# Batch 0's first attention part reordered around the transposes, q and k loaded and cast ahead of v, and feed-forward units metered by a carried credit

## The chip, the cores and the metric

The kernel runs on one core of a Trainium2 chip. The metric is the device time of one execution in microseconds; the time before is the median of three runs.

## The reference, cut to what matters

```python
def _attn_ref(q, k, v, is_retrieval, n_sink, window):      # 4 batches, 8 heads, 768 positions, depth 64
    scores = scale * np.matmul(q, k.transpose(0, 1, 3, 2))
    ...
    stream_keep = causal & (is_sink | in_win)              # 4 sinks, window 64
    mask = np.where(retr[0, :, 0, 0, None, None], full_mask, stream_mask)
    ...
    return np.matmul(a, v).astype(np.float32)              # a: softmax of the masked scores

def _moe_ref(x, w_in, w_out, alpha):                       # 3072 tokens, 512 -> 2048 -> 512
    h = x @ w_in
    g = np.maximum(h, 0.0) + alpha * np.minimum(h, 0.0)
    return (g @ w_out).astype(np.float32)
```

Heads 0, 2 and 6 are retrieval heads (causal mask), the other five are streaming heads (sinks and window). The attention output, heads side by side, is the x of the feed-forward part.

## The kernel before, in words

Every engine executes its instructions in the order in which the source emits them; the order is written by hand and nothing reorders it.

Attention is cut into segments of one batch and two heads. Batch 0 is split: segments 0 to 3 (kind "a", "part one") cover its first 512 positions, segments 4 to 7 (kind "b") the other 256. Segments 8 to 19 (kind "all") are the head pairs of batches 1 to 3. The fourth pair of each batch is two streaming heads, the other pairs one of each kind.

One segment goes like this. `load(n)` issues the DMAs of q, k and v (float32). `cast(n)` makes bf16 copies on POOL: `qb`, `kb` and, for v, `vb`, whose column of ones and empty tile `clear_v` has set. `Tq` and `Tk` transpose q and k on PE into one PSUM bank each, from which ACT (q of part one) or DVE (k, in one copy for a retrieval head, in three for a streaming head) copies them to `qT` and `kT`. The padding of `kT` is zeroed at the start by `clear_k`, each buffer on an engine of its own. `S_retr` and `S_stream` are the score pieces: matmuls into one of two score banks, then the exponential on ACT into `eR` or `eS`. In part one the mask is added on PE, by matmuls with `nmr` and `nms`; later DVE multiplies it in afterwards, with `mr`, `ms` and `ms5`. `AV(n, hh)` multiplies with `vb` and DVE divides (`rcp`, then `xn`); `X(n)` transposes the result, and DVE copies it to `xT`.

PSUM has eight banks: two for scores (`sc`), two for `AV` (`pav`), three for the feed-forward part (`mm0` to `mm2`) and a single one, `tr`, for all of `Tq`, `Tk` and `X`.

The feed-forward part is cut into units. `P1(t, f)` computes 128 of the 2048 hidden features of token tile t (512 or 256 tokens): four matmuls, a Relu on ACT (`neg`), and one DVE instruction (`g`). `P2(t, s, u)` is a quarter of the second product: four matmuls of 512 columns.

The program: loads 0 to 3; constants and clears; `cast(0)`, `Tq(0)`, `Tk(0)`; casts 1 to 3 on POOL with the issues of the weight loads `load_w_in(0..3)` and `load_w_out` between and behind them; the pieces of part one; P1 of token tile 0 (its last pair's share as soon as `X(3)` has run). Then the pieces of segments 4 to 19 follow, and after each piece as many units as a meter allows. A stage of the meter ends where a batch's last `xT` is due, and the units of the next tokens come in: tile 1 during segments 8 to 11, tiles 2 and 3 during 12 to 15, tiles 4 and 5 during 16 to 19. Tiles 6 and 7 run at the end. The meter before, with `left` the number of pieces to the end of the stage:

```python
budget = sum(c for c, _ in units) / left
while units and budget >= units[0][0] / 2:
    c, u = units.pop(0)
    budget -= c
    u()
```

Of the kernel before, what the change touches and what calls it, by code (L numbers as in the profile page):

```python
# [9 lines left out]
ALU = mybir.AluOpType  # L10
# [4 lines left out]
def kernel(  # L15
# [13 lines left out]
    nc = tc.nc  # L29
    B, H, S, D = q.shape  # L30
# [73 lines left out]

    def load(n, k_eng=None):
        sg, s = SEGS[n], n % NF
        base = (sg.b * H + sg.heads[0]) * S * D
        for src, dst, eng in ((q, qf[s], nc.sync), (k, kf[s], k_eng or nc.sync)):
            if sg.kind == "all":
                eng.dma_start(dst.rearrange("p h i d -> p (h i) d"),  # L110
                              dram(src, base, [[D, 128], [128 * D, 12], [1, D]]))
            else:

                T = (sg.q1 - sg.q0) // 128
                eng.dma_start(dst[:, :, 0:T, :].rearrange("p h i d -> p h (i d)"),
                              dram(src, base + sg.q0 * D, [[T * D, 128], [S * D, 2], [1, T * D]]))
        for hh, h in enumerate(sg.heads):
            lo, hi = sg.v_tiles(h)
            hi = min(hi, 6)
            o = (sg.b * H + h) * S * D  # L120
            step = 128 if RETR[h] else 124
            nc.sync.dma_start(vf[s][:, lo:hi, hh, :],
                              dram(v, o + lo * step * D, [[D, 128], [step * D, hi - lo], [1, D]]))
            if not RETR[h] and sg.kind != "a":
                nc.sync.dma_start(vf[s][0:24, 6, hh, :], dram(v, o + 744 * D, [[D, 24], [1, D]]))

    natq, natk = {}, {}

    def cast(n):
        sg, s = SEGS[n], n % NF  # L130
        vv = vb[sg.seq % NV]
        T = (sg.q1 - sg.q0) // 128
        if sg.kind == "b":
            natq[n], natk[n] = nat_b[0][sg.c], nat_b[1][sg.c]
        else:
            natq[n] = work.tile([128, 6, 128], bf16, tag="qb", name="qb")
            natk[n] = work.tile([128, 6, 128], bf16, tag="kb", name="kb")
        nc.gpsimd.tensor_copy(natq[n][:, 0:T, :].rearrange("p i (h d) -> p h i d", h=2), qf[s][:, :, 0:T, :])  # L138
        nc.gpsimd.tensor_copy(natk[n][:, 0:T, :].rearrange("p i (h d) -> p h i d", h=2), kf[s][:, :, 0:T, :])
        (la, ha), (lb, hb) = [sg.v_tiles(h) for h in sg.heads]  # L140
        if sg.kind == "all" or (la, ha) == (lb, hb):
            nc.gpsimd.tensor_copy(vv[:, lb:hb, :, 0:D], vf[s][:, lb:hb])
        else:
            nc.gpsimd.tensor_copy(vv[:, la:ha, 0, 0:D], vf[s][:, la:ha, 0])
            nc.gpsimd.tensor_copy(vv[:, lb:hb, 1, 0:D], vf[s][:, lb:hb, 1])
        for hh, h in enumerate(sg.heads):
            if not RETR[h]:
                lo, hi = sg.v_tiles(h)
                lo = max(lo, 1)
                vh = vv[0:NSINK, :, hh, 0:D]  # L150
                nc.gpsimd.tensor_copy(vh[:, lo:hi, :], vh[:, 0:1, :].to_broadcast([NSINK, hi - lo, D]))

    load(0, nc.scalar)
    load(1, nc.scalar)
    alpha_r = wpool.tile([16, 128], fp32, name="alpha_r")
    nc.scalar.dma_start(alpha_r, moe_alpha.rearrange("(a p) -> a p", p=128))
    load(2, nc.scalar)
    load(3)

# [11 lines left out]
    nmr = const.tile([128, 5, 144], bf16, name="nmr")  # L171
    nms = const.tile([128, 2, 192], bf16, name="nms")

# [26 lines left out]

    clear_k(nc.scalar, 1)
    clear_k(nc.vector, 0)
    nc.vector.memset(qT[0][:, SPLIT:S + 32], 0.0)
    nc.vector.tensor_copy(ms[:, 1, :], ms[:, 0, :])
    nc.vector.tensor_scalar(nms, ms, -1.0, 30000.0, op0=ALU.add, op1=ALU.mult)
    nc.vector.tensor_scalar(nmr, mr, -1.0, 30000.0, op0=ALU.add, op1=ALU.mult)
    for e in eR:
        nc.vector.memset(e[:, 1292:1612], 1.0)
        nc.vector.memset(e[:, E_R - 128:E_R], 1.0)
    clear_e(nc.vector, eS[0])  # L210
    for i in range(NV):
        clear_v(nc.vector, i)
    for i in range(1, NK):
        nc.vector.memset(qT[i][:, SPLIT:S + 32], 0.0)
    clear_k(nc.gpsimd, 2)
    clear_k(nc.scalar, 3)

# [12 lines left out]

    def T_bank(nat, n):
        tr = ps.tile([128, 1024], bf16, tag="tr", name="tr")
        for i in range(n):
            nc.tensor.transpose(tr[:, 128 * i:128 * (i + 1)], nat[:, i, :], ident)  # L234
        return tr

    def Tq(n):
        sg = SEGS[n]
        T = (sg.q1 - sg.q0) // 128
        tr = T_bank(natq.pop(n), T)  # L240
        dst = qT[sg.seq % NK][:, sg.q0:sg.q1]
# [6 lines left out]
    def Tk(n):  # L248
        sg = SEGS[n]
        T = (sg.q1 - sg.q0) // 128  # L250
        tr = T_bank(natk.pop(n), T)
        for hh, h in enumerate(sg.heads):
# [75 lines left out]
    def S_stream(n, hh, m):  # L328
# [18 lines left out]
        for j, a, z in parts + extra:  # L347
            nc.tensor.matmul(sc[:, o:o + z - a], kt[:, 128 * j:128 * (j + 1)],  # L348
                             qt[:, 124 * j + a:124 * j + z], start=True, stop=not on_pe)
            if on_pe:  # L350
                nc.tensor.matmul(sc[:, o:o + z - a], ident, nms[:, 0, a:z], start=False, stop=True)
            o += z - a
# [92 lines left out]

    def seg_pieces(n):
        sg = SEGS[n]
        parts = []
        for hh, h in enumerate(sg.heads):
            fn, m = (S_retr, sg.n_r) if RETR[h] else (S_stream, sg.n_s)  # L450
            parts.append([lambda m=m, hh=hh, fn=fn: fn(n, hh, m) for m in range(m)])
        sa, sb = parts

# [6 lines left out]

    cast(0)
    Tq(0)
    Tk(0)
    cast(1)
    load_w_in(0)
    clear_e(nc.gpsimd, eS[1])
    cast(2)
    for i in range(1, 4):
        load_w_in(i)
    cast(3)  # L470
    clear_e(nc.gpsimd, eS[2])
    clear_k(nc.gpsimd, 4)
    for i in range(NF):
# [6 lines left out]
    for n in range(8, 8 + NF):  # L480
        load(n)
    for n in range(3):
        for piece in seg_pieces(n)[0]:
            piece()
        if n == 0:

            tra = ps.tile([128, 16], fp32, tag="tr", name="tra")
            nc.tensor.transpose(tra, alpha_r, ident_f)
            nc.vector.tensor_scalar(oma, tra, -1.0, 1.0, op0=ALU.mult, op1=ALU.add)

            nc.vector.tensor_copy(ms5[:, 0, :], ms[:, 0, :])
            nc.vector.tensor_copy(ms5[:, 1, 0:148], ms[:, 0, 0:148])
            nc.vector.tensor_copy(ms5[:, 1, 148:192], ms[:, 0, 0:44])
            nc.vector.memset(ms5[0:NSINK, 1, 148:152], 0.0)
    for piece in seg_pieces(3)[0]:
        piece()
    P1(0, 0, range(3))
# [27 lines left out]
    fills = [i for i, (_, _, ready) in enumerate(pieces) if ready]  # L525
    units = p1_units(0, range(13, 16)) + p2_units(0)
    for i, (pre, piece, ready) in enumerate(pieces):
# [4 lines left out]
        if ready and i < fills[-1]:  # L532
            for _, u in units:
                u()
            units = []
            for t in ready:
                units += p1_units(t) + p2_units(t)
            continue
        if i == fills[-1]:
            break  # L540
        budget = sum(c for c, _ in units) / left
        while units and budget >= units[0][0] / 2:
# [49 lines left out]
```

## Time and profile before

| | |
|---|---|
| median of 3 runs | 276.46 us (276.16 to 276.47) |
| profiled execution | 276.85 us, its span 274.5 us |
| PE busy | 241.5 us (88% of the span) |
| DVE busy | 180.5 us (66%) |
| ACT busy | 144.8 us (53%) |
| POOL busy | 67.6 us (25%) |

The span runs from the first to the last instruction; the rest of the execution's time lies around it. Busy time is the time in which an engine had an instruction running; a releaser in square brackets is what ended the idle time before an instruction, inferred from semaphore events.

### The profile page before, as it was taken

Reading aid. Unit: us, or ns where it says so; the run is one execution under the profiler, and the core shown is the slowest. Engines: PE = TensorE matmul, PEld = TensorE weight load, DVE = VectorE, ACT = ScalarE, POOL = GpSimd, SP = SyncE. Lnnn points to the kernel's source line nnn. Section 1 sums busy time; section 2 is a strip of 40 time slices with the busy share of each in tenths; the row PEclk is TensorE's granted clock in tenths of the full one; section 3 lists DMA queues with packets and bytes.
Section 4 is the critical chain, followed back from the end, with each engine's and each line's share of the span. In section 5 each row is a group of like instructions: output and inputs, shape, how many; then the busy total and the mean of one; then the engine's idle time right before and its main releaser. Section 6 shows DMA issues by size and latency. Waiting matters only on the chain.

```text
span 274.5 us, 5621 instructions
## 1 busy us (share of the span) xinstructions
PE 241.5 (88%) x2113; PEld 150.6 (55%) x2139; DVE 180.5 (66%) x481; ACT 144.8 (53%) x307; POOL 67.6 (25%) x122
## 2 busy tenths in 40 slices
PE   0486789897998588999999899999998999999994
PEld 0365534554586465555556765555555854456551
DVE  7566578745699876699642986798436955873320
ACT  5445367553476443667534644776345744654421
POOL 7899225500451244050401312220000000000000
PEclk9999999999999989999999999999999999999998
DMA  7999999999995954961021101000111011000111
GB/s 215 275 215 213 208 224 221 221 213 250 244 251 112 175 111 101 212 146 31 0 79 39 41 0 41 38 2 1 41 76 39 4 40 39 0 2 38 76 40 76
DMA packets 75274, 29.84 MB, mean 109 GB/s; under 512 B 63968, under 2 KB 72176, under 8 KB 75248
## 3 DMA queue, kind: packets, MB, share of 16 engines
q1 hardware_dynamic: 70176, 24.51, 40.4%
q0 software_dynamic: 4224, 4.19, 9.1%
q10 hardware_dynamic: 848, 0.79, 0.9%
q8 instruction: 16, 0.26, 0.4%
q14 instruction: 10, 0.08, 0.1%
HBM read 27.39 MB, written 6.29 MB: 123 GB/s over the span
## 4 chain that ended last, share of the span: by engine, by line
PE 68%; DVE 16%; ACT 5%; DMA 3%; issue 2%; POOL 2%; SPq 1%; ACTq 0%; POOLq 0%; DVEq 0%
PE mm L414 25%; PE mm L431 20%; PE sc L431 7%; PE pav L379 5%; DVE g L421 5%; PE tr L234 3%; PE sc L316 3%; DVE xn L386 3%; PE tr L394 2%; PE sc L348 2%; ACT eR L323 2%; DMA vf<-in_v_dram 2%; ACT neg L420 2%; DVE eS L360 2%; DMA kf<-in_k_dram 2%
## 5 line engine op out<-in xcount | busy, mean ns | idle before, releaser
L414 PE MATMUL mm<-xT,w_in_b 128*128 128x256 bf16 (+1 forms) x503 | 98.2, 325 | 4.6 <-DVE g L421 3.3
L421 DVE SCALAR_TENSOR_TENSOR g<-neg,oma,mm 128x512 bf16<-128x512 f32 (+1 forms) x128 | 77.1, 611 | 23.3 <-ACT neg L420 19.9
L420 ACT ACTIVATE neg<-mm 128x512 f32<-128x512 f32 (+1 forms) x128 | 62.4, 492 | 41.8 <-PE mm L414 37.1
L431 PE MATMUL mm<-w_out_b,g 128*128 128x512 bf16 x274 | 71.5, 379 | 0.8
L414 PEld LDWEIGHTS <-w_in_b 128*128 128x128 bf16 x512 | 47.8, 98 | 34.2 <-issue 5.8
L323 ACT ACTIVATE eR<-sc 128x455 bf16<-128x455 f32 (+5 forms) x72 | 38.9, 551 | 23.2 <-PE sc L316 19.4
L431 PEld LDWEIGHTS <-g 128*128 128x128 bf16 x384 | 34.9, 98 | 26.7
L355 ACT ACTIVATE eS<-sc 128x384 bf16<-128x384 f32 x60 | 29.1, 490 | 33.4 <-PE sc L348 27.0
L138 POOL CAST qb<-qf 128x768 bf16<-128x768 f32 (+1 forms) x16 | 12.4, 777 | 84.9 <-PE tr L234 69.7
L316 PE MATMUL sc<-qT,kT 128*128 128x268 bf16 (+16 forms) x141 | 26.8, 274 | 2.1 <-DVE kT L270 1.5
L326 DVE TENSOR_TENSOR eR<-eR,mr 128x128 bf16<-128x128 bf16 (+4 forms) x60 | 14.3, 255 | 16.8 <-ACT eR L323 16.6
L360 DVE TENSOR_TENSOR eS<-eS,ms 128x384 bf16<-128x384 bf16 x50 | 18.4, 373 | 10.4 <-ACT eS L355 10.2
L431 PE MATMUL sc<-w_out_b,g 128*128 128x512 bf16 x93 | 22.9, 379 | 0.2
L386 DVE TENSOR_TENSOR xn<-pav,rcp 128x448 bf16<-128x448 f32 (+2 forms) x40 | 21.8, 544 | 1.4
L348 PE MATMUL sc<-qT,kT 128*128 128x192 bf16 (+4 forms) x150 | 21.3, 234 | 0.3 <-DVE kT L277 0.3
L316 PEld LDWEIGHTS <-kT 128*128 128x128 bf16 x141 | 12.4, 101 | 11.5 <-DVE kT L270 2.0
L435 ACT COPY ot<-mm 128x512 f32<-128x512 f32 x18 | 10.6, 586 | 14.1 <-PE mm L431 14.1
L348 PEld LDWEIGHTS <-kT 128*128 128x128 bf16 x150 | 14.0, 99 | 6.7 <-DVE kT L277 0.4
L379 PEld LDWEIGHTS <-eS 128*128 128x128 bf16 x270 | 11.8, 99 | 7.9 <-DVE eS L360 3.3
L379 PE MATMUL pav<-vb,eS 128*128 128x65 bf16 x270 | 13.5, 195 | 2.4 <-DVE eS L360 2.0
L396 DVE COPY xT<-tr 128x768 bf16<-128x768 bf16 (+2 forms) x20 | 9.5, 475 | 9.3 <-PE tr L394 9.3
L234 PE MATMUL tr<-ident,qb 128*128 128x128 bf16 x88 | 8.3, 233 | 7.9 <-POOL qb L138 5.3
(79 smaller groups left out, 207.4 us busy)
## 6 DMA issues: line engine op xcount, KB each, us to landing
out_dram<-ot SPq DMA_DIRECT2D x24, 256.0 KB
qf<-in_q_dram SPq DMA_DIRECT2D x12, 384.0 KB
kf<-in_k_dram SPq DMA_DIRECT2D x12, 384.0 KB
vf<-in_v_dram SPq DMA_DIRECT2D x24, 192.0 KB
w_in_b<-in_moe_w_in_dram POOLq DMA_DIRECT2D x4, 512.0 KB, 7.5
w_out_b<-in_moe_w_out_dram POOLq DMA_DIRECT2D x4, 512.0 KB, 12.0
qf<-in_q_dram SPq DMA_DIRECT2D x4, 256.0 KB
vf<-in_v_dram SPq DMA_DIRECT2D x5, 160.0 KB
```

What stands on the lines that cost most here:

```text
L234: nc.tensor.transpose(tr[:, 128 * i:128 * (i + 1)], nat[:, i, :], ident)
L316: nc.tensor.matmul(sc[:, a - lo:z - lo], kt[:, 128 * j:128 * (j + 1)], qt[:, c:c + z - a], start=True, stop=not masked)
L323: nc.scalar.activation(e[:, lo:hi], sc[:, 0:hi - lo], AF.Exp, scale=scale)
L348: nc.tensor.matmul(sc[:, o:o + z - a], kt[:, 128 * j:128 * (j + 1)], qt[:, 124 * j + a:124 * j + z], start=True, stop=not on_pe)
L355: nc.scalar.activation(two, sc[:, 0:384].rearrange("p (s c) -> p s c", c=192), AF.Exp, scale=scale)
L360: nc.vector.tensor_tensor(two, two, ms5 if first == 4 else ms, op=ALU.mult)
L379: nc.tensor.matmul(pav[:, i, :], e[:, o:o + 128], vv[:, j, hh, :], start=(m == 0), stop=(m == len(terms) - 1))
L386: nc.vector.tensor_tensor(xn[n][:, lo:hi, 64 * hh:64 * hh + 64], pav[:, lo:hi, 0:D], rcp[:, lo:hi].to_broadcast([128, hi - lo, D]), op=ALU ...
L414: nc.tensor.matmul(psg[:, 0:w], w_in_b[:, a, 128 * f:128 * (f + 1)], xT[:, c, o:o + w], start=(c == 0), stop=(c == 3))
L420: nc.scalar.activation(neg[:, 0:w], psg[:, 0:w], AF.Relu, scale=-1.0)
L421: nc.vector.scalar_tensor_tensor(g_buf[t % 2][:, f, 0:w], neg[:, 0:w], oma[:, f:f + 1], psg[:, 0:w], op0=ALU.mult, op1=ALU.add)
L431: nc.tensor.matmul(po[t], g_buf[t % 2][:, f, 128 * s:128 * (s + 1)], w_out_b[:, f, :], start=(f == 0), stop=(f == 15))
```

## The change

1. **Order of part one.** `Tq(n+1)` and `Tk(n+1)` come after the second score piece of segment n; `AV(n, 0)` comes last in segment n, `AV(n-1, 1)` after two score pieces of segment n, `X(n-1)` behind the first piece of the second head.
2. **Banks.** In part one `Tq` takes the bank `mm0` and `Tk` the bank `mm1`; `tr` serves `X` alone.
3. **Loads and casts.** q and k are loaded and cast apart from v: `load_qk(0)`, `(1)`, `load_v(0)`, `load_qk(2)`, and so on; k of segment 2 is issued on SP instead of ACT. The first weight load is issued after the v cast of segment 1, the last two after the v cast of segment 3.
4. **Clears and constants.** `kT` buffers 1, 2 and 3 change engines (1 from ACT to DVE, 2 from POOL to ACT, 3 from ACT to POOL); ACT's clear, and DVE's clears of `vb`, `eS[0]` and `qT[1..4]`, move behind `Tk(0)`; the second half of `ms` and with it half of `nms` leaves the start, and `ms`, `ms5` are completed after part one.
5. **Meter.** The budget is carried from piece to piece.

```diff
-    load(0, nc.scalar)
-    load(1, nc.scalar)
+    load_qk(0, nc.scalar)
+    load_qk(1, nc.scalar)
 ...
-    load(2, nc.scalar)
-    load(3)
+    load_v(0)
+    load_qk(2, nc.sync)
+    load_v(1)
+    load_qk(3, nc.sync)
+    load_v(2)
+    load_v(3)
...
-    clear_k(nc.scalar, 1)
     clear_k(nc.vector, 0)
     nc.vector.memset(qT[0][:, SPLIT:S + 32], 0.0)
-    nc.vector.tensor_copy(ms[:, 1, :], ms[:, 0, :])
-    nc.vector.tensor_scalar(nms, ms, -1.0, 30000.0, op0=ALU.add, op1=ALU.mult)
+    clear_k(nc.gpsimd, 3)
     nc.vector.tensor_scalar(nmr, mr, -1.0, 30000.0, op0=ALU.add, op1=ALU.mult)
+    nc.vector.tensor_scalar(nms, ms[:, 0, :], -1.0, 30000.0, op0=ALU.add, op1=ALU.mult)
+    clear_k(nc.vector, 1)
     for e in eR:
         nc.vector.memset(e[:, 1292:1612], 1.0)
         nc.vector.memset(e[:, E_R - 128:E_R], 1.0)
-    clear_e(nc.vector, eS[0])
-    for i in range(NV):
-        clear_v(nc.vector, i)
-    for i in range(1, NK):
-        nc.vector.memset(qT[i][:, SPLIT:S + 32], 0.0)
-    clear_k(nc.gpsimd, 2)
-    clear_k(nc.scalar, 3)
...
-        tr = T_bank(natq.pop(n), T)
+        tr = T_bank(natq.pop(n), T, "mm0" if sg.kind == "a" else "tr")
...
-        tr = T_bank(natk.pop(n), T)
+        tr = T_bank(natk.pop(n), T, "mm1" if sg.kind == "a" else "tr")
...
-    cast(0)
+    cast_qk(0)
     Tq(0)
     Tk(0)
-    cast(1)
+    clear_k(nc.scalar, 2)
+    for i in range(NV):
+        clear_v(nc.vector, i)
+    clear_e(nc.vector, eS[0])
+    cast_qk(1)
+    cast_v(0)
+    clear_e(nc.gpsimd, eS[1])
+    cast_qk(2)
+    cast_v(1)
     load_w_in(0)
-    clear_e(nc.gpsimd, eS[1])
-    cast(2)
-    for i in range(1, 4):
-        load_w_in(i)
-    cast(3)
+    cast_qk(3)
+    cast_v(2)
+    load_w_in(1)
     clear_e(nc.gpsimd, eS[2])
+    cast_v(3)
+    load_w_in(2)
+    load_w_in(3)
...
-    for n in range(3):
-        for piece in seg_pieces(n)[0]:
+    for i in range(1, NK):
+        nc.vector.memset(qT[i][:, SPLIT:S + 32], 0.0)
+    for n in range(4):
+        sa, sb = seg_scores(n)
+        first = [lambda: AV(n - 1, 1)] if n else []
+        if n < 3:
+            first += [lambda: Tq(n + 1), lambda: Tk(n + 1)]
+        seq = sa[:2] + first + sa[2:] + sb[:1]
+        seq += ([lambda: X(n - 1)] if n else []) + sb[1:] + [lambda: AV(n, 0)]
+        for piece in seq:
             piece()
...
-            nc.vector.tensor_copy(ms5[:, 0, :], ms[:, 0, :])
-            nc.vector.tensor_copy(ms5[:, 1, 0:148], ms[:, 0, 0:148])
-            nc.vector.tensor_copy(ms5[:, 1, 148:192], ms[:, 0, 0:44])
-            nc.vector.memset(ms5[0:NSINK, 1, 148:152], 0.0)
-    for piece in seg_pieces(3)[0]:
-        piece()
+    nc.vector.tensor_copy(ms[:, 1, :], ms[:, 0, :])
+    nc.vector.tensor_copy(ms5[:, 0, :], ms[:, 0, :])
+    nc.vector.tensor_copy(ms5[:, 1, 0:148], ms[:, 0, 0:148])
+    nc.vector.tensor_copy(ms5[:, 1, 148:192], ms[:, 0, 0:44])
+    nc.vector.memset(ms5[0:NSINK, 1, 148:152], 0.0)
...
-        budget = sum(c for c, _ in units) / left
+        if not ready:
+            budget += (sum(c for c, _ in units) - budget) / left
```

## Rows read from the trace of the kernel before

**Rows 1.** The page: its span, and the DMA engines' busy tenths in 40 slices.
```profile
span 274.5 us, 5621 instructions
...
DMA  7999999999995954961021101000111011000111
```

**Rows 2.** Busy time by stretch: start:end and length, engines (instructions), granted clock, DMA.
```profile
10.10:16.00 5.90, 5.08 (x43) 4.22 (x43) 2.85 (x9) 2.60 (x6) 5.77 (x13) 1.00 1.23 256
16.00:21.20 5.20, 3.90 (x56) 3.08 (x56) 2.94 (x11) 3.08 (x7) 5.14 (x12) 1.00 1.24 208
21.20:27.20 6.00, 3.87 (x60) 3.03 (x58) 3.31 (x12) 3.25 (x8) 5.53 (x14) 1.00 1.23 213
27.20:34.30 7.10, 5.20 (x66) 3.74 (x68) 4.35 (x13) 2.45 (x8) 1.89 (x7) 1.00 1.22 207
...
74.40:90.00 15.60, 14.44 (x186) 11.88 (x183) 13.90 (x40) 11.77 (x31) 5.66 (x8) 1.00 0.91 183
90.00:100.00 10.00, 6.88 (x92) 5.07 (x89) 7.70 (x25) 4.45 (x9) 2.80 (x5) 0.83 0.62 117
100.00:113.30 13.30, 11.81 (x118) 7.52 (x120) 9.78 (x28) 5.74 (x13) 4.34 (x6) 1.00 0.76 164
113.30:151.70 38.40, 38.02 (x309) 21.87 (x312) 25.42 (x62) 22.75 (x46) 7.94 (x11) 1.00 0.30 75
```

**Rows 3.** Timeline up to the first scores: start, length, engine, instruction, idle before.
```profile
2.95 1.79 DVE L204 COPY ms<-ms 128x192 bf16<-128x192 bf16 x1
3.05 1.63 POOL L189 MEMSET kT<- 128x896 bf16 x2
4.21 3.45 ACT L187 CAST kT<-zero 128x896 bf16<-128x896 f32 x4
...
5.17 0.65 POOL L139 CAST kb<-kf 128x512 bf16<-128x512 f32 x1
...
7.57 0.57 ACT L245 COPY qT<-tr 128x512 bf16<-128x512 bf16 x1
...
8.20 0.59 PE L234 MATMUL tr<-ident,kb 128*128 128x128 bf16 x4 [2.29 <-POOL vb L145]
...
9.40 0.62 DVE L270 COPY kT<-tr 64x512 bf16<-64x512 bf16 x1
...
10.08 0.54 PE L316 MATMUL sc<-qT,kT 128*128 128x430 bf16 x1 [1.30 <-DVE kT L270]
```

**Rows 4.** Timeline: weight issues, transposes around segment 1's middle, last P1 share.
```profile
14.78 2.23 POOL L223 DMA_DIRECT2D w_in_b<-in_moe_w_in_dram  x3
...
17.86 0.45 PE L394 MATMUL tr<-ident,xn 128*128 128x128 bf16 x5
...
18.83 0.38 PE L234 MATMUL tr<-ident,qb 128*128 128x128 bf16 x4 [0.52 <-POOL vb L142]
...
19.89 0.38 PE L234 MATMUL tr<-ident,kb 128*128 128x128 bf16 x4 [0.67 <-ACT qT L245]
...
34.28 0.81 PE L414 MATMUL mm<-xT,w_in_b 128*128 128x512 bf16 x3 [0.51 <-DVE xT L396]
```

**Rows 5.** Groups by line: count, busy us, mean ns of one, idle before.
```profile
L189 DVE MEMSET kT<- 128x448 uint32 x2 | 0.9, 432 | 0.1
...
L206 DVE TENSOR_SCALAR nmr<-mr 128x720 bf16<-128x720 bf16 x1 | 0.8, 751 | 0.0
...
L208 DVE MEMSET eR<- 128x320 bf16 x2 | 0.7, 325 | 0.0
...
L205 DVE TENSOR_SCALAR nms<-ms 128x384 bf16<-128x384 bf16 x1 | 0.6, 577 | 0.0
...
L492 DVE COPY ms<-ms 128x148 bf16<-128x148 bf16 x1 | 0.5, 506 | 0.0
...
L209 DVE MEMSET eR<- 128x128 bf16 x2 | 0.3, 165 | 0.0
```

**Rows 6.** The tile `w_in_b`: time from the issue of its four loads to landing.
```profile
DMA to landing us min/median/max: 6.0/7.5/10.5
```

More of the change, by code (lines that the diff above doesn't have):

```diff
@@ L103, in dram, with load, load_qk @@
         return bass.AP(t.tensor, t.offset + offset, dims)
-    def load(n, k_eng=None):
+    def load(n):
+        load_qk(n, nc.sync)
+        load_v(n)
+    def load_qk(n, k_eng):
         sg, s = SEGS[n], n % NF
         base = (sg.b * H + sg.heads[0]) * S * D
-        for src, dst, eng in ((q, qf[s], nc.sync), (k, kf[s], k_eng or nc.sync)):
+        for src, dst, eng in ((q, qf[s], nc.sync), (k, kf[s], k_eng)):
             if sg.kind == "all":
@@ L116, in load, with load_v @@
                               dram(src, base + sg.q0 * D, [[T * D, 128], [S * D, 2], [1, T * D]]))
+    def load_v(n):
+        sg, s = SEGS[n], n % NF
         for hh, h in enumerate(sg.heads):
@@ L129, in cast, with cast_qk @@
     def cast(n):
+        cast_qk(n)
+        cast_v(n)
+    def cast_qk(n):
         sg, s = SEGS[n], n % NF
-        vv = vb[sg.seq % NV]
         T = (sg.q1 - sg.q0) // 128
@@ L139, in cast, with cast_v @@
         nc.gpsimd.tensor_copy(natk[n][:, 0:T, :].rearrange("p i (h d) -> p h i d", h=2), kf[s][:, :, 0:T, :])
+    def cast_v(n):
+        sg, s = SEGS[n], n % NF
+        vv = vb[sg.seq % NV]
         (la, ha), (lb, hb) = [sg.v_tiles(h) for h in sg.heads]
@@ L171 @@
     nmr = const.tile([128, 5, 144], bf16, name="nmr")
-    nms = const.tile([128, 2, 192], bf16, name="nms")
+    nms = const.tile([128, 192], bf16, name="nms")
     nc.gpsimd.affine_select(ms[:, 0, :], ones.to_broadcast([128, 192]), pattern=[[-1, 192]], base=63,
@@ L228, in load_w_out, with T_bank @@
                             moe_w_out[512 * n:512 * (n + 1), :].rearrange("(a p) f -> p a f", p=128))
-    def T_bank(nat, n):
-        tr = ps.tile([128, 1024], bf16, tag="tr", name="tr")
+    def T_bank(nat, n, tag):
+        tr = ps.tile([128, 1024], bf16, tag=tag, name="tr")
         for i in range(n):
@@ L350, in S_stream @@
             if on_pe:
-                nc.tensor.matmul(sc[:, o:o + z - a], ident, nms[:, 0, a:z], start=False, stop=True)
+                nc.tensor.matmul(sc[:, o:o + z - a], ident, nms[:, a:z], start=False, stop=True)
             o += z - a
@@ L443, in p2_units, with seg_scores @@
         return [(1, lambda s=s, u=u: P2(t, s, u)) for s in range(TOK[t][1] // 128) for u in range(4)]
-    def seg_pieces(n):
+    def seg_scores(n):
         sg = SEGS[n]
@@ L451, in seg_pieces @@
             parts.append([lambda m=m, hh=hh, fn=fn: fn(n, hh, m) for m in range(m)])
-        sa, sb = parts
+        return parts
+    def seg_pieces(n):
+        sa, sb = seg_scores(n)
         prev = [lambda: AV(n - 1, 1)] if n not in (0, 4) else []
@@ L481 @@
         load(n)
-    for n in range(3):
-        for piece in seg_pieces(n)[0]:
+    for i in range(1, NK):
+        nc.vector.memset(qT[i][:, SPLIT:S + 32], 0.0)
+    for n in range(4):
+        sa, sb = seg_scores(n)
+        first = [lambda: AV(n - 1, 1)] if n else []
[4 more added lines that the diff above has]
+        for piece in seq:
             piece()
@@ L525 @@
     fills = [i for i, (_, _, ready) in enumerate(pieces) if ready]
-    units = p1_units(0, range(13, 16)) + p2_units(0)
+    units, budget = p1_units(0, range(13, 16)) + p2_units(0), 0
     for i, (pre, piece, ready) in enumerate(pieces):
@@ L534 @@
                 u()
-            units = []
+            units, budget = [], 0
             for t in ready:
```

## The prediction

> **What bounds the kernel now.** I read the page first, for where the time lies, then the table of busy time by stretch, then the timeline of the stretches in which PE has gaps. From the middle of the kernel on, PE sets the pace: from 113.30 to 151.70 it is busy 38.02 of 38.40 us [rows 2]. Nothing that leaves PE's work alone can gain there. Two places are different.
>
> The first is part one, up to 34.28, where the last share of token tile 0's first P1 starts [rows 4]. Scores begin only at 10.08 [rows 3], and from 10.10 to 34.30 PE is idle 0.82, 1.30, 2.13 and 1.90 us, 6.15 us in all [rows 2]. POOL is nearly always busy up to 27.20, and the chain of waits runs over it, but I don't take POOL for the bound. It does work there that nobody waits for soon (clears, weight issues), and the waits in which PE stands are at the transposes.
>
> The second is the stage of segments 8 to 11, 74.40 to 113.30 (38.9 us). PE is idle 1.16 us in its first 15.6, 3.12 us in the middle 10 and 1.49 us in the last 13.3 [rows 2]. In the middle the granted clock is 0.83 on average: of the two levels, 2.4 and 1.2 GHz, the lower for 0.17 x 2 x 10 = 3.4 us. There the meter hands out nothing. The stage has 53 pieces and units worth 16 (sixteen P1 of 0.5, eight P2 of 1). 16/53 = 0.30 is over half of a P1, so the meter before gives one P1 after nearly every piece; the sixteen are gone after 20 pieces. The eight P2 then need a budget of 0.5, that is at most 16 pieces left. Seventeen pieces in between get none.
>
> **Part by part, first scores.** Before, `Tk(0)` writes into the same bank as `Tq(0)`, and so waits for ACT's copy of q, which starts at 7.57, because ACT zeroes `kT` from 4.21 to 7.66. The trace names a v cast as releaser of this wait of 2.29 us; by the times it is the copy, which ends at 8.14, just ahead of the transposes at 8.20 [rows 3]. The change gives `Tk` a bank and ACT nothing to do first. The k cast ends at 5.82, so k's transposes end near 5.82 + 0.59 = 6.41. Then DVE must be free. Its queue ahead of the k copy: `nmr` 0.75, half of `nms` 0.29, the moved `kT` clear 0.9, the `eR` memsets 0.7 + 0.3 [rows 5]. It starts at 3.05 with `nmr`. Lower bound: `nmr` runs at once and ends at 3.80, the queue at 5.99, and the copy starts at 6.41, 3.0 us before 9.40. Upper bound: `nmr` is held up by POOL's clear as the copy of `ms` is now (1.79 us, up to 4.74, where POOL's two memsets end at 4.68 [rows 3]; a similar copy later takes 0.51 [rows 5]). Then it ends at 5.43, the queue at 7.62, 1.8 us before 9.40. The situation is that of the row, so I take **1.8 us**.
>
> ACT's clear of buffer 2 and DVE's clears of `vb`, `eS` and `qT` now run behind `Tk(0)`. They cost nothing if PE's scores of segment 0 cover them; without cover they delay `kT` of segment 1, which is needed a whole segment later. The v cast waits for the first `vb` clear, but `AV(0, 0)` now comes last in segment 0.
>
> **Stalls inside part one.** In segment 1 the transposes of X, q and k follow each other through the one bank: q's wait 0.52 us for the copy out of X's bank, k's 0.67 us for ACT's copy of q; from 17.86 to 19.89 PE does hardly more than nine transposes [rows 4]. The two waits stand again in segment 2, the second alone in segment 0: 2 x 1.19 + 0.67 = 3.05 us. Separate banks remove them. The rest of the 6.15 us is mostly waiting for `xn` ahead of X; X moves behind a score piece, which covers part of it, and `Tk` moves far enough ahead for DVE's copies to be done before their scores. Bounds: 1.5 us if waits for a score bank or for DVE take the place of half of the bank's waits, 6.15 us if nothing takes it. I take **3.4 us**, the bank's waits and a little of the others.
>
> Against this stands the completion of `ms` and `ms5`. Four DVE copies of about 0.5 us [rows 5] leave segment 0 for a place ahead of the division of `AV(3, 1)`, on which X(3) and the P1 at 34.28 hang. Six P1 matmuls on PE run meanwhile (0.81 us for three [rows 4]), so 2.0 - 1.6 = 0.4 us shows, about **-0.5 us**. Bounds: 0 if DVE is early; 4 x 1.79 - 1.6 = 5.6 us lost if POOL holds up each copy.
>
> **Loads.** q and k of segment 3 are issued and cast earlier, v later; since v is needed only in `AV`, nothing waits. The moved `kf` issue on SP stands behind three v or q issues that ACT did not have, but its cast comes later than before in nobody's path. Weights: the last issue moves from 17.01 [rows 4] behind the casts of segment 3, some five POOL instructions of up to 0.65 us [rows 3]: at most 20.3, landing by 20.3 + 10.5 = 30.8 [rows 6]. P1 of tile 0 needs that last quarter only from its thirteenth feature block on, after 29.6 + 10 blocks. Hidden, then; the issue of SP's later loads hangs on a POOL memset that moves little. The DMA engines are full for the first thirty per cent of the span anyway [rows 1].
>
> **The meter.** Carrying the budget spreads the stage's units: by its arithmetic P1 after two pieces in three, and a P2 after every third piece from the middle on. Two effects. The lower clock in the middle goes: 3.4 us of it with PE busy 6.88/10 cost about 1.2 us. And the idle time: it is 0.06 and 0.09 us a piece where units are dense (20 and 16 pieces), 0.18 where there are none (17). If the spread stage has the dense rate, 53 x 0.075 = 4.0 us are left of 5.77; if idle falls in proportion to units (0.11 a piece at 0.30 units), 5.8, no gain. Bounds 0 and 1.2 + 2.7 = 3.9 us (the latter at 0.06); I take **2.2 us**. In the later stages the meter only moves units by a piece or so, while PE stays full: 0. The added condition on `ready` never decides, as the loop has gone on or ended before it.
>
> **Sum.** 1.8 + 3.4 - 0.5 + 2.2 = 6.9 us. The profiled execution took 276.85 us (span 274.5 and 2.35 around it), so 269.95; the median lies 0.39 lower, which gives **269.6 us**.
>
> **Rivals.** *Only part one gains*: DVE, busy 13.90 of 15.60 us where P1 units are dense [rows 2], is what limits the stage, and spreading moves idle time about. 276.5 - 4.7 = 271.8 us. For it speaks that DVE's masks come ahead of every `AV`; against it the low clock in the middle.
>
> *Weights or q, k, v become the bound of part one*: PE arrives early and waits for `w_in_b` or the casts. Part one's gain is lost, the meter's stays: 274.3 us. It decides once landing takes some 6 us longer than the 10.5 seen; the full DMA engines speak for it, the order of need against it.
>
> *More than forecast*: all bounds on the good side, 3.0 + 6.15 + 3.9 = 13.05; a little over half of the additional gain gives 265 us.
>
> *`ms` copies held up*: POOL is at work while DVE makes the four copies, and X(3) is 5.6 us late. 1.8 + 3.4 - 5.6 + 2.2 = 1.8 us gained, 274.7 us, or no change if the meter gives nothing. The Trainium skill (SBUF — State Buffer, section "SBUF: two separate sides") says that POOL and certain DVE instructions share a port pair, and that the later one waits for a whole instruction of the other; the trace agrees at the 1.79 us copy. Against this rival: by then POOL has mostly casts that wait for data, not memsets.
>
> *Slower: the clock falls in the stage of segments 8 to 11.* The units that now come in two dense groups are thinned out; PE could have gaps all along and be granted 1.2 GHz in much of the stage. The row in the middle shows that this happens [rows 2]. One us at the lower level with PE as the limit costs 0.5 us, so it outweighs part one's 4.7 us from 9.4 us of low clock beyond the present 3.4. With half of the stage, some 19 us, the loss is 8 - 4.7 = 3.3 us: 279.8 us. Against it: an even spread leaves PE busy about 31.9 of 36.7 us, 87%, near the 89% of the stretch from 100.00, which had the full clock. The Trainium skill (TensorE: Matmul & The Clock Gate, section "Part 1: The HAM clock gate") describes the lower level as the default that activity lifts; the trace agrees in that the clock fell in the only stretch without units.
>
> **How the numbers follow.** Forecast 0.56, only part one 0.15, weights 0.08, more 0.09, `ms` held up 0.06, clock 0.06. A measurement of this kernel tells changes over 0.2% (0.55 us) from none. Faster: all but the clock and half of the `ms` case, 0.91; same 0.03; slower 0.06. The range of 8 in 10 leaves out the clock, most of "more" and of `ms`: 266.0 to 274.0 us.
>
> **What would show it.** First scores near 8.3; k's transposes of segment 0 right behind the k cast; no idle time at `Tq`, `Tk` from other copies; the P1 share now at 34.28 near 29.6; PE idle in the stage of segments 8 to 11 about 4.8 us without a stretch of low clock. I would be wrong if DVE's queue in front of the first k copy is longer than worked out, if score banks hold PE up in part one, or if P1 of tile 0 waits for weights.

## The result and the profile after

The changed kernel takes 266.33 us (median of 4 runs, 265.64 to 267.19) against 276.47 us before in the same comparison: a ratio of 0.9635, with an interval of 0.9597 to 0.9673. The forecast was 269.6 us, 266.0 to 274.0. So the direction was right and 10.1 us were gained where 6.9 were expected; the measured time lies 0.3 us inside the lower end of the range.

The page after, its span and the clock granted to PE in 40 slices:

```profile
span 263.8 us, 5619 instructions
...
PEclk9999999999999999999999999999999999999999
```

The table of busy time by stretch after, with stretches chosen as those of [rows 2] were: segments 0 to 3 and the first P1 shares, then the stage of segments 8 to 11 and the next one. The last line is part one in a single stretch.

```profile
7.90:12.40 4.50, 4.49 (x43) 3.75 (x43) 3.87 (x22) 3.37 (x8) 3.26 (x9) 1.00 1.22 318
12.40:15.60 3.20, 3.13 (x58) 2.74 (x57) 3.07 (x10) 2.57 (x8) 3.14 (x7) 1.00 0.60 116
15.60:18.90 3.30, 3.30 (x62) 2.80 (x59) 3.17 (x12) 2.90 (x8) 3.17 (x9) 1.00 1.10 179
18.90:22.20 3.30, 2.73 (x49) 2.37 (x47) 2.42 (x10) 2.05 (x7) 3.30 (x7) 1.00 1.14 177
22.20:26.00 3.80, 2.66 (x23) 1.33 (x23) 3.05 (x10) 0.34 (x2) 3.80 (x10) 1.00 1.24 205
...
66.40:103.30 36.90, 31.53 (x388) 23.49 (x389) 30.58 (x91) 21.68 (x52) 12.99 (x17) 1.00 0.98 227
103.30:161.00 57.70, 56.96 (x511) 35.59 (x516) 42.00 (x107) 33.82 (x73) 13.03 (x17) 1.00 0.19 53
...
7.90:25.96 18.06, 16.27 (x220) 12.96 (x222) 15.58 (x60) 11.22 (x28) 16.63 (x37) 1.00 1.08 208
```

Behind the bounds of a stretch, the first two numbers carry the argument: its length and PE's busy time in it. In segments 0 to 2 the two are now all but equal, so PE hardly waits there any more. From the first scores to the last P1 share part one took 24.20 us before, with 18.05 us of PE work and 6.15 us idle [rows 2 to 4]; it takes 18.06 us after, with 16.27 us of PE work and 1.79 us idle. Two things have shrunk: the idle time by 4.36 us, and the busy time of the same work by 1.78 us.

The timeline up to the scores of segments 0 and 1, which answers to [rows 3]:

```profile
3.14 1.74 DVE L222 TENSOR_SCALAR nmr<-mr 128x720 bf16<-128x720 bf16 x1
...
5.95 0.61 PE L245 MATMUL tr<-ident,kb 128*128 128x128 bf16 x4
...
6.04 0.59 ACT L256 COPY qT<-tr 128x512 bf16<-128x512 bf16 x1 [2.40 <-PE tr L245]
...
7.23 0.62 DVE L281 COPY kT<-tr 64x512 bf16<-64x512 bf16 x1
...
7.91 0.54 PE L327 MATMUL sc<-qT,kT 128*128 128x430 bf16 x1 [1.35 <-DVE kT L281]
...
12.42 0.36 PE L327 MATMUL sc<-qT,kT 128*128 128x430 bf16 x1
```

The transposes of k follow the cast, ACT copies q at once, and the first scores come at 7.91 instead of 10.08. The last two lines are the same matmul of 430 columns in segments 0 and 1: 0.54 us, then 0.36 us. That is PE at its lower level of 1.2 GHz and then at 2.4 GHz: in the run with a single bank, below, this matmul takes 0.55 us at 20.25 us, where the granted clock is 0.50 (from 20 to 21 us). Here the column of the granted clock says 1.00 for both stretches, so the lengths of like matmuls have to show the level. They fall near 11.7 us after the change and near 16.9 us before, where the first matmul of segment 1 was still long:

```profile
16.02 0.54 PE L316 MATMUL sc<-qT,kT 128*128 128x430 bf16 x1
```

The timeline around the transposes of part one, and its end, which answers to [rows 4]:

```profile
13.18 0.39 PE L245 MATMUL tr<-ident,qb 128*128 128x128 bf16 x4
13.40 0.39 PE L245 MATMUL tr<-ident,kb 128*128 128x128 bf16 x4
...
14.51 0.45 PE L405 MATMUL tr<-ident,xn 128*128 128x128 bf16 x5
...
24.99 0.45 PE L405 MATMUL tr<-ident,xn 128*128 128x128 bf16 x5 [0.61 <-DVE xn L397]
25.96 0.81 PE L425 MATMUL mm<-xT,w_in_b 128*128 128x512 bf16 x3 [0.52 <-DVE xT L407]
```

The transposes of q and k stand 0.22 us apart and wait for nothing. The last P1 share comes at 25.96 instead of 34.28: 8.32 us, of the 10.7 us by which the span got shorter. X(7) keeps 7.99 us of them (66.26 against 74.25), X(11) is 9.88 us earlier (102.88 against 112.76), so the stage between the two has gained 1.9 us. The rest of the kernel adds 0.8 us.

### The profile page after: what moved, and what is told of

Read it like the earlier page. It is cut to its first block, busy times and chain, and to the rows that moved or that the text cites. A ratio compares the mean times of both kernels' runs of the same rounds, so it can differ in the third digit from the quotient of the medians.

```text
span 263.8 us, 5619 instructions
## 1 busy us (share of the span) xinstructions
PE 238.1 (90%) x2112; PEld 148.3 (56%) x2139; DVE 181.3 (69%) x483; ACT 142.2 (54%) x305; POOL 68.1 (26%) x122
## 4 chain that ended last, share of the span: by engine, by line
PE 63%; DVE 16%; DMA 7%; POOL 6%; ACT 4%; issue 3%; SPq 0%; POOLq 0%; ACTq 0%; DVEq 0%
PE mm L442 21%; PE mm L425 20%; PE sc L442 8%; DVE g L432 5%; PE pav L390 4%; DMA vf<-in_v_dram 4%; DMA kf<-in_k_dram 3%; PE sc L327 3%; PE tr L245 3%; DVE xn L397 2%; PE sc L359 2%; PE tr L405 2%; DVE eS L371 2%; ACT eR L334 2%; DVE eR L337 1%
## 5 line engine op out<-in xcount | busy, mean ns | idle before, releaser
L334 ACT ACTIVATE eR<-sc 128x455 bf16<-128x455 f32 (+5 forms) x72 | 38.7, 552 | 18.8 <-PE sc L327 17.5
L327 PE MATMUL sc<-qT,kT 128*128 128x268 bf16 (+16 forms) x141 | 25.8, 268 | 1.6 <-DVE kT L281 1.6
L149 POOL CAST kb<-kf 128x768 bf16<-128x768 f32 (+1 forms) x16 | 12.6, 786 | 11.2 <-PE tr L245 7.5
```

The lines of the kernel that those rows point to most:

```text
L327: nc.tensor.matmul(sc[:, a - lo:z - lo], kt[:, 128 * j:128 * (j + 1)], qt[:, c:c + z - a], start=True, stop=not masked)
L334: nc.scalar.activation(e[:, lo:hi], sc[:, 0:hi - lo], AF.Exp, scale=scale)
```

## The experiments

The start of the last P1 share ("the share" below; 34.28 before, 25.96 after) measures part one in one execution, without what comes later, which the median also holds. It depends on the execution too: where PE's clock rises at another time, the share moves. Two runs below with the same part one, both with late masks, have it at 25.51 and 26.03 us, with the 430 columns of segment 1 at 0.36 and at 0.54 us. So differences of half a microsecond in it say little.

**The meter undone.**

```diff
-        if not ready:
-            budget += (sum(c for c, _ in units) - budget) / left
+        budget = sum(c for c, _ in units) / left
```

> The changed kernel with the meter of before (the budget starts anew at each piece). If spreading the units is worth what the two traces suggest (stage of segments 8 to 11: 38.5 us before, 36.6 after), the time rises by 1.9 to 2.2 us to about 268.4, and the stretch without units shows a mean granted clock below 1 again. If DVE sets the pace of that stage whatever the meter does, it rises by 0.5 us at most, to 266.8.

Measured: 268.18 us (267.78 to 269.46), ratio 0.9694 [0.9653, 0.9734], 1.85 us more than with the change. The stage of segments 8 to 11 as a stretch:

```profile
66.70:105.10 38.40, 32.90 (x386) 23.98 (x383) 31.50 (x91) 21.52 (x52) 12.81 (x17) 0.96 0.89 207
```

From X(7) to X(11) it takes 38.4 us, as before (38.5; 36.6 after), with a mean granted clock of 0.96. Against the changed kernel PE is busy 1.4 us longer for the same work, and idle 5.5 instead of 5.4 us. So in this stage the meter is worth about what was forecast, but nearly all of it is PE's busy time, with the clock, and hardly any the idle time. The next two stages also go back to their lengths of before: from X(11) to X(15) 58.5 us (58.5 before, 57.7 after), from X(15) to X(19) 57.2 us (57.2 before, 56.5 after).

**All transposes of part one in one bank.**

```diff
-        tr = T_bank(natq.pop(n), T, "mm0" if sg.kind == "a" else "tr")
+        tr = T_bank(natq.pop(n), T, "tr")
...
-        tr = T_bank(natk.pop(n), T, "mm1" if sg.kind == "a" else "tr")
+        tr = T_bank(natk.pop(n), T, "tr")
```

> The changed kernel with all transposes of part one in the one bank tr again; order, loads, clears and meter stay changed. The prediction put 3.05 us of part one down to waits for that bank: if so, PE stands 2.5 to 3.5 us more at the transposes and the time is about 269.4. If the new order has already put enough work between them, so that only k's wait for the copy of q is left (0.67 us, three times), it is 268.3; if the copies are hidden altogether, 266.5.

Measured: 272.62 us (270.81 to 273.61), ratio 0.9839 [0.9783, 0.9894], and the share at 34.21, as late as before. From its timeline:

```profile
6.68 0.59 PE L245 MATMUL tr<-ident,kb 128*128 128x128 bf16 x4 [0.67 <-ACT qT L256]
...
16.27 0.38 PE L245 MATMUL tr<-ident,kb 128*128 128x128 bf16 x4 [0.67 <-ACT qT L256]
...
18.38 0.60 PE L405 MATMUL tr<-ident,xn 128*128 128x128 bf16 x5 [1.08 <-DVE kT L288]
...
20.25 0.55 PE L327 MATMUL sc<-qT,kT 128*128 128x430 bf16 x1
...
34.21 0.81 PE L425 MATMUL mm<-xT,w_in_b 128*128 128x512 bf16 x3 [0.52 <-DVE xT L407]
```

And segment 2, then part one in a single stretch, from its table by stretch:

```profile
20.25:27.00 6.75, 4.84 (x61) 4.08 (x59) 3.50 (x11) 3.07 (x8) 6.51 (x14) 0.75 1.22 202
...
8.04:34.21 26.17, 20.66 (x221) 16.30 (x222) 15.47 (x60) 11.59 (x28) 19.28 (x44) 0.87 1.13 205
```

This is more than any of the expected outcomes, although each wait is about as long as expected: 0.67 us for q's copy, 1.1 to 1.2 us where X now waits for k's copies. Idle time is 5.5 us, 3.7 more than after; but PE's busy time for the same work is 20.66 us, 4.4 more than after. PE's clock had come up (the transposes at 16.27 us take 0.38 us) and fell again: the five transposes at 18.38 us take 0.60 us instead of 0.45, and at 20.25 us the 430 columns take 0.55 us. In this execution the waits cost their own length and, in PE's clock, as much again. It is the slowest of the four: two were granted 0.986 on average and took 273.5 and 273.6 us, the other two 0.999 and took 270.8 and 271.8. So some 2 us of the loss depend on the execution.

**The order of the pieces undone.** Part one runs the pieces of `seg_pieces` as before.

```diff
...
-        seq = sa[:2] + first + sa[2:] + sb[:1]
-        seq += ([lambda: X(n - 1)] if n else []) + sb[1:] + [lambda: AV(n, 0)]
-        for piece in seq:
+        for piece in seg_pieces(n)[0]:
```

> The changed kernel with the order of the pieces of part one as before; banks, loads, clears and meter stay changed. If the banks are what removed the idle time of PE in part one, the time rises by 0.5 us at most (266.8). If the order did it, because X waits for xn, and scores wait for kT, when they are close behind, 2 to 4 us come back (268.3 to 270.3).

Measured: 267.08 us (266.93 to 268.51), ratio 0.9662 [0.9615, 0.9709]; the share at 27.58, 1.62 us later. Two lines of its timeline, the scores of segment 1 and X:

```profile
12.95 0.36 PE L327 MATMUL sc<-qT,kT 128*128 128x430 bf16 x1
...
18.61 0.45 PE L405 MATMUL tr<-ident,xn 128*128 128x128 bf16 x5 [0.45 <-DVE xn L397]
```

This lies between the two outcomes. X waits for `xn` again (0.45 us here), but the matmuls are short from segment 1 on. The order is worth less than the banks: 1.6 us in part one. In the median it is 0.75 us, which the spread alone would not show (265.64 to 267.19 us with the order).

**q, k and v together.** Loads, casts and weight issues stand in the order of before.

```diff
...
-    cast_qk(1)
     cast_v(0)
+    cast(1)
...
-    cast_qk(2)
-    cast_v(1)
...
+    cast(2)
...
```

> The changed kernel with q, k and v loaded and cast together, segment by segment, and the weight issues between them as before. The prediction costed this part at nothing, because v is needed only in AV: then 266.3 to 266.8. The rival: the v cast of segment 0 waits on POOL for DVE's clear (it ends near 9.1 us), and the q and k casts of segment 1 stand behind it, so that the transposes of segment 1, at 8.8 us now, come about 2 us later and part one with them: 268.3, and more if PE's clock rises later too.

Measured: 268.33 us (267.76 to 269.91), ratio 0.97 [0.9655, 0.9746]; the share at 28.62, 2.66 us later. Its timeline in segment 1 (in brackets the wait and what ended it):

```profile
10.61 0.61 PE L244 MATMUL tr<-ident,qb 128*128 128x128 bf16 x4 [1.59 <-POOL qb L148]
...
14.75 0.54 PE L326 MATMUL sc<-qT,kT 128*128 128x430 bf16 x1
```

The rival holds: segment 1's transposes wait 1.59 us for the q cast. It stands on POOL behind v's cast, which itself waits 2.83 us for DVE's clear of `vb`, one of the clears that this change moved. The first matmul of segment 1 is long again.

**PE kept busy ahead of the first scores, in both kernels.** Constant matmuls into an unused bank, 34 ahead of `Tq(0)` (24 more ahead of `Tk(0)` in the kernel before) and 12 behind `Tk(0)`:

```diff
+    warm = ps.tile([128, 512], fp32, tag="pav1", name="warm")
+    for _ in range(34):
+        nc.tensor.matmul(warm[:, 0:128], ident, ident, start=True, stop=True)
...
```

> The changed kernel with 34 matmuls of a constant ahead of the first transposes and 12 behind them, into a bank that is not in use, so that PE is busy from 1.4 us on. PE works through segment 0 without a gap now (7.9 to 12.4 us), and its matmuls have the lengths of 1.2 GHz until about 11.1. If PE's clock is what is left there, about 1.3 us are gained: 265.0. If DVE's queue is the limit (the clears that stand ahead of segment 1's kT copy end at 11.4, so the scores of segment 1 can't start before 12.1), 0.3 us: 266.0.

> The kernel before with constant matmuls ahead of, between and behind its first transposes (34, 24, 12), so that PE is busy from 1.4 us until its first scores. If the lower clock of PE's first scores (full length until about 16.9) is a cost of its own, the 1.8 us of PE busy time that part one lost with the change come here too: 274.7, with the matmuls of segment 0 at half their length. If PE waits for others in segment 0 anyway, shorter matmuls only lengthen the waits: 276.0 or more.

With the change: 265.38 us (265.25 to 266.64), ratio 0.9582 [0.9531, 0.9633], which overlaps that without; the share at 25.94, the same. Its timeline, the scores of segments 0 and 1:

```profile
7.90 0.36 PE L327 MATMUL sc<-qT,kT 128*128 128x430 bf16 x1 [0.89 <-DVE kT L281]
...
12.13 0.36 PE L327 MATMUL sc<-qT,kT 128*128 128x430 bf16 x1 [0.75 <-DVE kT L281]
```

The matmuls of segment 0 are short, and then segment 1 waits for its `kT` copy until 12.13: DVE's queue is the limit of segment 0 now. From 7.90 us to the share PE is busy 14.85 us, 1.42 less than without the constant matmuls, and idle 1.40 us more: shorter matmuls came back as waits. Before the change: 277.96 us, 0.4% slower (1.0039 [1.0009, 1.0069]), with the share at 35.76, 1.5 us later. Its timeline at the scores of segment 1 and X(0), and its table by stretch behind them (length, PE's busy time, and third from the end the granted clock):

```profile
14.98 0.36 PE L316 MATMUL sc<-qT,kT 128*128 128x430 bf16 x1
...
17.81 0.45 PE L394 MATMUL tr<-ident,xn 128*128 128x128 bf16 x5 [1.32 <-DVE xn L386]
```

```profile
16.00:21.30 5.30, 2.78 (x27) 2.25 (x27) 2.67 (x8) 1.60 (x4) 5.24 (x12) 0.72 1.24 208
21.30:27.30 6.00, 4.81 (x55) 4.01 (x53) 2.78 (x9) 3.21 (x7) 5.55 (x14) 0.68 1.23 215
```

This is the second outcome, and more. Segment 1's scores come 1.04 us earlier than in the kernel before (14.98 against 16.02), but X(0) does not (17.81 against 17.86): it waits 1.32 us for `xn`, beside 0.51 and 0.67 us at the one bank. So PE is idle 2.5 of 5.3 us, and then the granted clock falls, to 0.72 and 0.68 in the two stretches. The high clock at the start gained nothing here, and it did not last through the waits.

**The banks alone, in the kernel before.** The edit of the single-bank run the other way round.

> The kernel before with one edit: in part one Tq writes to the bank mm0 and Tk to mm1. By the sum of the waits (3.05 us inside part one, and the first k transposes, which no longer wait for ACT) 273.0 or a little less. If the waits also keep PE's clock down, as the run with a single bank in the changed kernel suggests (its scores of segment 2 still have the length of 1.2 GHz at 20.3 us, and all of part one's gain is gone), the matmuls get short several us earlier and it is 270 to 272.

Measured: 273.98 us (273.89 to 275.1), ratio 0.9891 [0.984, 0.9942]; the share at 31.21, 3.07 us earlier, with first scores at 10.08 as before. Its timeline at X(0), and part one as a stretch:

```profile
17.81 0.45 PE L394 MATMUL tr<-ident,xn 128*128 128x128 bf16 x5 [1.04 <-DVE xn L386]
```

```profile
10.08:31.21 21.13, 17.07 (x222) 13.70 (x223) 14.24 (x42) 11.35 (x27) 17.42 (x40) 1.00 1.23 222
```

The gain equals the sum of the waits, 3.05 us, but not for that reason alone. PE's idle time fell by 2.09 us only (6.15 to 4.06): X(0) now waits 1.04 us for `xn`, because DVE is making the copies of `ms5` then. The other 0.98 us is PE's busy time (18.05 to 17.07), as the matmuls get short near 15.3 us instead of 16.9.

**The clears undone.** ACT clears ahead of its copy of q, DVE clears `vb`, `eS` and `qT` ahead of the first k copy:

```diff
+    clear_k(nc.scalar, 1)
...
-    clear_k(nc.gpsimd, 3)
...
-    clear_k(nc.vector, 1)
...
+    clear_e(nc.vector, eS[0])
+    for i in range(NV):
+        clear_v(nc.vector, i)
+    for i in range(1, NK):
+        nc.vector.memset(qT[i][:, SPLIT:S + 32], 0.0)
+    clear_k(nc.gpsimd, 2)
+    clear_k(nc.scalar, 3)
...
```

> The changed kernel with the clears as before: ACT zeroes two kT buffers ahead of its first copy of q, DVE clears vb, eS and qT ahead of the first k copy, POOL buffer 2. The prediction's sum for the first scores was 1.8 us, the trace says 2.2 (10.08 to 7.91). If that is carried to the end, 268.1 to 268.5. If it is made up for inside part one, because the same clears then don't stand ahead of segment 1's kT copy and v's cast, 266.5 to 267.5.

Measured: 267.02 us (266.46 to 267.51), ratio 0.963 [0.9582, 0.9678]; the share at 27.12. The first scores in its timeline:

```profile
9.45 0.54 PE L333 MATMUL sc<-qT,kT 128*128 128x430 bf16 x1 [2.90 <-DVE kT L287]
```

The scores begin 1.54 us later and the share 1.16 us: part of it is made up for. The medians differ by 0.7 us, with ranges that overlap. The remaining 0.6 us from 9.45 to the 10.08 of before is the copy of `ms`, which these kernels no longer have at the start.

**Banks, casts and late masks, with the old order, clears and meter.** The edits of three runs above together (order, clears and meter undone).

> The changed kernel with the order of part one, the clears and the meter as before; what stays changed is the two banks, q and k loaded and cast ahead of v, and the masks completed after part one. The kernel before with the banks alone had its last P1 share at 31.21 us and a median of 273.98. If loading and casting q and k first is worth 2 us by itself, as undoing it in the changed kernel cost, the share comes near 28.5 and the time is 271.5 to 272. If it only matters once the first scores are earlier and the transposes follow them sooner (with the old order and clears the transposes of segment 1 wait for no cast), the share stays near 31.2 to 31.6 and the time near 274.0.

Measured: 271.65 us (271.3 to 272.05), ratio 0.9804 [0.9766, 0.9841]; the share at 29.28, between the two. X(0) in its timeline, without a wait:

```profile
16.29 0.45 PE L411 MATMUL tr<-ident,xn 128*128 128x128 bf16 x5
```

Neither reason fits. No transposes waited for a cast in the run with the banks alone, so a cast that came sooner can't have ended a wait of PE and given the 1.93 us. 0.63 of them are the earlier first scores; most of the others are at this line: X(0) no longer waits its 1.04 us. The `ms5` copies have left segment 0, and DVE makes `xn` 1.5 us earlier. No run moved these copies alone.

**The masks completed still later.**

```diff
...
     X(3)
+    nc.vector.tensor_copy(ms[:, 1, :], ms[:, 0, :])
+    nc.vector.tensor_copy(ms5[:, 0, :], ms[:, 0, :])
     for f in range(3):
         P1(0, f, range(3, 4))
+    nc.vector.tensor_copy(ms5[:, 1, 0:148], ms[:, 0, 0:148])
...
```

> The changed kernel with the DVE copies that complete ms and ms5 moved behind X(3), two ahead of the last P1 share's units and two behind them. The prediction put 0.5 us on these copies standing ahead of the division of AV(3, 1). By it the wait of X(3) for xn (0.61 us) falls to about 0.17 and the last P1 share starts at about 25.5 instead of 25.96: 265.9, if DVE has room for them while PE does P1. If they delay P1's DVE instructions as much there, no change: 266.3.

Measured: 265.9 us (265.5 to 266.91), ratio 0.9591 [0.9548, 0.9633]. The end of part one in its timeline:

```profile
24.54 0.45 PE L405 MATMUL tr<-ident,xn 128*128 128x128 bf16 x5 [0.17 <-DVE xn L397]
25.51 0.81 PE L425 MATMUL mm<-xT,w_in_b 128*128 128x512 bf16 x3 [0.52 <-DVE xT L407]
```

And what follows part one, from its table by stretch:

```profile
26.00:36.40 10.40, 9.31 (x36) 3.82 (x36) 7.29 (x13) 5.94 (x11) 3.22 (x11) 0.84 1.19 205
```

The share comes 0.45 us earlier, as worked out; the medians differ by as much, which their spread alone would not show (the ranges overlap). In the profiled execution, the slowest of the four, the gain was lost again: the granted clock was 0.84 in the P1 that follows, and X(7) came at 67.66 instead of 66.26.

**A bank for Tk in the later segments.** `Tk` of segments 5 to 12, then, with the late masks, of 5 to 8, takes the next feed-forward bank:

```diff
-        tr = T_bank(natk.pop(n), T, "mm1" if sg.kind == "a" else "tr")
+        tr = T_bank(natk.pop(n), T, "mm1" if sg.kind == "a" else mm_tag() if 4 < n < 13 else "tr")
...
```

> The changed kernel, with Tk of segments 5 to 12 also writing to a bank of its own, the next one of the three feed-forward banks. In the trace of the changed kernel these transposes still wait for the copy of q out of tr in six places between 41 and 98 us, 4.07 us in all, and the run with a single bank in part one says that such waits cost at least their length. If so, 262 to 263. If DVE, busy 30.6 of 36.9 us in the stage of segments 8 to 11, sets the pace there, the waits only move: 265.3 to 266.3.

> The changed kernel with the masks completed behind X(3), and Tk's own bank only in segments 5 to 8. With it in segments 5 to 12 the stage up to X(7) got 1.2 us shorter (X(7) at 65.09 instead of 66.26) and the next one 2.1 us longer, because DVE, which frees the banks, is the limit there. If that is the reason, leaving segments 9 to 12 at tr keeps the first and avoids the second: 1.2 us and the 0.45 us of the masks less than the changed kernel, 264.7. If the time won ahead of X(7) is lost again whatever bank follows, 265.9 as with the masks alone.

Segments 5 to 12: 267.61 us (266.49 to 269.61), ratio 0.9665 [0.9609, 0.9721], not faster than the change. Its table by stretch, for the stage of segments 4 to 7 and that of segments 8 to 11:

```profile
36.40:65.20 28.80, 25.80 (x241) 15.03 (x244) 19.74 (x65) 14.32 (x33) 12.10 (x21) 1.00 1.04 228
65.20:103.90 38.70, 31.78 (x382) 23.43 (x383) 33.77 (x91) 21.60 (x52) 12.63 (x17) 1.00 0.98 228
```

The first stage is 1.2 us shorter, the second longer (38.7 us against 36.6). There the transposes of k no longer wait (2.8 us after the change), but other waits of PE take their place. In its timeline a P1 waits for a bank until DVE has copied k out of it, and an `AV` for masked scores:

```profile
74.05 0.59 PE L390 MATMUL pav<-vb,eS 128*128 128x65 bf16 x9 [0.87 <-DVE eS L371]
...
82.28 0.61 PE L428 MATMUL mm<-xT,w_in_b 128*128 128x256 bf16 x4 [0.65 <-DVE kT L275]
```

In this stage the first kind is 0.9 us in all, the second, waits of `AV` for `eS` and `eR`, 3.7 us (0.4 after the change). DVE is busy 33.8 of 38.7 us, 3.2 more than after the change with as many instructions. Nearly all of that is in its multiplications by `mr`, whose group on the page after the change and on the page of this run reads:

```profile
L337 DVE TENSOR_TENSOR eR<-eR,mr 128x128 bf16<-128x128 bf16 (+4 forms) x60 | 14.3, 257 | 16.6 <-ACT eR L334 16.5
...
L337 DVE TENSOR_TENSOR eR<-eR,mr 128x128 bf16<-128x128 bf16 (+4 forms) x60 | 17.6, 311 | 16.4 <-ACT eR L334 16.2
```

Six of them grew. Those of 144 columns took 0.96 us each instead of 0.22, at moments when POOL casts k and v, which it now starts sooner, as k's transposes free `kb` sooner. At 90.31 us two of them take 1.57 us, beside POOL's casts of k and v from 90.09 to 91.79; after the change two take 0.37 us at 89.50, ahead of the cast of k at 90.01. So `Tk` without its wait moved POOL's casts onto DVE's masks, and as far as this trace shows, that is what made DVE the limit. No run held the casts back to test it.

Segments 5 to 8 with the late masks: 264.69 us (264.4 to 265.37), ratio 0.9565 [0.9541, 0.9589], and the fastest version of this study. X(7) and X(11) in its timeline:

```profile
65.31 0.33 PE L405 MATMUL tr<-ident,xn 128*128 128x128 bf16 x3
...
101.91 0.56 PE L405 MATMUL tr<-ident,xn 128*128 128x128 bf16 x7
```

The stage between them takes 36.6 us, as in the changed kernel. The median is the 264.7 us forecast, but the trace shows only part of the sum behind it. In the profiled execution the clock rose later and the share came at 26.03 us, no earlier than in the changed kernel, and X(7) is 0.95 us earlier, not 1.65. The spans agree with the smaller gain: 262.6 to 263.3 us, against 263.8 to 264.0 us in three of the changed kernel's four executions.

## Why the prediction was right in direction and too small in size, point by point

Four steps lead from before to after. PE's busy and idle time count from the first scores to the share:

| kernel | first scores | share | PE busy | PE idle |
|---|---|---|---|---|
| before | 10.08 | 34.28 | 18.05 | 6.15 |
| with the banks | 10.08 | 31.21 | 17.07 | 4.06 |
| with the casts and the late masks too | 9.45 | 29.28 | 17.20 | 2.63 |
| with the clears too | 7.90 | 27.58 | 17.09 | 2.59 |
| with the order too (the change) | 7.91 | 25.96 | 16.27 | 1.79 |

**First scores** (1.8 us forecast): 2.17 us, by the mechanism worked out. DVE's queue was the limit, and `nmr` was held up beside POOL's clear (1.74 us). It ended at 4.88, right after the clear, not 0.75 us behind it, as the upper bound had it. Against that, the half of `nms` took 0.60 us, not 0.29: it took as long as the whole had.

**Stalls inside part one** (3.4 us, less 0.5 for the masks): this is the term that was mis-sized. From the first scores to the share 6.14 us were gained, 4.36 of idle time and 1.78 of PE's busy time, which the sum did not have at all. The mechanism, separate banks, was right, and with the banks alone in the kernel before the sum of the waits seems to be met (3.07 against 3.05 us). That is partly luck: the wait of X(0) took the place of 1.04 us of the bank's waits, and 0.98 us of busy time made up for it. "A little of the others", 0.35 us, was too small: the order brought 1.62 us, and the step with the casts and late masks 1.30 us beyond its earlier first scores.

A wait was priced at its length. The single-bank run shows what that leaves out: in its profiled execution PE's clock fell behind the waits, and its busy time grew by 4.4 us where its idle time grew by 3.7. But a higher clock is no gain of its own. With PE kept busy early, the shorter matmuls came back as idle time in the changed kernel, and in the kernel before the clock fell again among the waits. So how much of the 1.78 us would have been gained without the shorter waits is not shown.

**Masks** (-0.5 us): 0.45 us at the place named, where the wait of X(3) fell from 0.61 to 0.17 us. Not counted was the gain where they came from: segment 0's `ms5` copies held up X(0), which waited 1.04 us in the run with the banks alone.

**Loads and casts** (0): wrong. Once the first scores are early and `Tq(1)` follows the second score piece, q's cast behind v's would be late by 1.59 us, and the share by 2.66, because v's cast waits for a clear that the change moved. "Nothing waits" held for the kernel before and not for the changed one. Weights, as forecast, were waited for by nobody in part one.

**Meter** (2.2 us): the stage of segments 8 to 11 gained 1.9 us. Its two parts were to be 1.2 us of clock and 1.0 of idle time; against the run with the old meter PE's busy time fell by 1.4 us and its idle time by 0.1. So the total came out near by luck: the larger part from the clock made up for the idle time, which stayed.

**Later stages** (0): X(11) to the end gained 0.8 us, and this is the meter too. The next two stages gained 0.8 and 0.7 us and the end lost 0.6; with the old meter all three have their lengths of before again, within 0.1 us. That the meter "only moves units by a piece or so" there was not the whole of it. Undone, the meter cost 1.85 us in the median and 2.9 us between the two profiled executions.

**Rivals.** "Only part one gains" falls with the undone meter, late weights with the trace. The copies of the masks took 0.38 to 0.77 us each, not 1.79. The clock did not fall in the stage of segments 8 to 11: 1.00, with 5.4 us idle. "More than forecast", at 265 us, is the rival that came nearest. By its own words it should have said about 266.3 us: half of the additional gain of 13.05 - 6.9 = 6.15 us is 3.1 us; the 265 us printed take three quarters of it.

## What to carry to other kernels

Look at the lengths of like matmuls before and behind a wait, not only at the idle column: where they grow, the wait costs more than its length. But shorter matmuls are worth something only where PE is not waiting for another engine anyway. A sum that comes out right can hide two errors; check idle and busy time apart. A step that costs nothing in the old order must be checked against the order that the other steps make: PE waited for no cast in the old order, and the same casts would have cost 2 us in the new one. A bank of its own removes a wait and lets everything behind it start sooner; ask what that meets, as here POOL's casts met DVE's masks.

## What the runs showed of the hardware that was not expected

PE's clock fell beside waits of half a microsecond to 1.3 us each. Started early at 2.4 GHz in the kernel before, it was granted 0.72 and 0.68 on average in the stretches from 16.0 to 27.3 us, where PE was idle 2.5 of 5.3 and 1.2 of 6.0 us. The same waits don't always bring it down: in P1 behind part one (from 26.0 to 36.4 us) the changed kernel was granted 1.00, and the run with the late masks, with a shorter wait ahead of it, 0.84. Executions of one program differ in this as well: of the changed kernel's four, three were granted 1.000 on average, with spans of 263.8 to 264.0 us, and one 0.994, with 265.5.

DVE's multiplications of two tiles in SBUF, 0.22 us each for 144 columns, took 0.96 us each where they ran beside POOL's casts.
